# A fused attention and gated-MLP block: normalizing the first tokens on GpSimd, raw spatial weights on its queue, and one weight's parts made early

## The chip, the cores and the metric

The kernel runs on one NeuronCore of a Trainium2 chip. Its engines are TensorE (PE, with weight loads listed apart as PEld), VectorE (DVE), ScalarE (ACT), GpSimd (POOL) and SyncE (SP), which here only issues DMAs. The metric is the device time of one execution in microseconds (us), lower is better. It was 1884.51 us before the change: the median of 3 runs from 1882.85 to 1885.61.

## The reference

```python
x = A_x                                  # 1 x 2048 x 512, fp32
xn = layernorm(x)
# attention, 32 heads of 16
qkv = (xn @ wqkv) -> q, k, v
p = softmax(q k^T / sqrt(16));  a = (p v) @ wo
# gMLP, F = 1792, half 896
z = gelu(xn @ w_in);  z1, z2 = z[:, :896], layernorm(z[:, 896:])
g = w_sp @ z2 + b_sp[:, None]            # w_sp is 2048 x 2048
return x + a + (z1 * g) @ w_out
```

## The kernel before

All products are done with fp32 values split in two parts of a shorter format (the high part, a cast, and the low part, the rest after a subtraction), in three matmuls. Weights come as a raw fp32 tile by DMA, and `weight` makes the parts on GpSimd: `tensor_copy` (L282) and `tensor_sub` (L284). Parts, transposed x and other large tiles share a ring of 19 buffers ("big"); three more hold parts that are on their way out ("hilo").

**The start** is written out by hand. The 16 token tiles are four groups g. For each group `norm_x` computes mean and variance on DVE and normalizes in place (L327, ACT), `turn_x` transposes on PE (L333) and makes the parts xnT on ACT (L71) and DVE (L233), `qk_first` makes q and k of the first heads (L236 to L238), `v_tile` makes one token tile's v, and `load_stacks` loads q and k back in the layout of the scores. The parts of the v weights are cast by an early DMA and a DVE subtraction. xnT is stored to DRAM (xscr) by GpSimd's queue (L155).

**The loop** takes the 16 pairs of heads p, four column groups c and sixteen key tiles kt: 1024 steps. Each has a score matmul (S, L1095), its exponential on ACT (pf<-sl), a maxima matmul (M, L1109) for the next pair, its reduction on DVE (L811), and values (V, L1192), which come in blocks: after 8 scores, the 32 matmuls of 8 steps. There are 128 blocks. The gaps of PE are filled with dense work (D, L1154), two matmuls at a time on the two halves of the array, called a dense pair here. Where no dense work is ready, a filler pair (L1168) that computes nothing takes its place. The kind of pair is chosen by a planner at the end of the function, which runs when the program is built, has a clock of its own and writes out a fixed order for each engine:

```python
        queue = [v_rest(), qk_rest(), z2_all(), z1_all(), spatial(), mlp_out(), attn_out()]
        order = [(p, c, kt) for p in range(NP) for c in range(NG) for kt in range(NT)]
```

The dense queue is in that order: remaining v, remaining q and k, z2 and z1 of the gMLP, the spatial product (weights `wsp`, operand `zs` loaded from z2scr), the gMLP's output, and the attention's output (`op` and `ohl` from oscr, weights `wo`). Generators for the other engines yield an engine's letter ("G" for GpSimd) and an estimated time. `prepare` starts one `weight` per tile; `move` issues a DMA from SP, and `store` one from GpSimd in the start and from SP afterwards. `load_stacks` loads the next pair's q and k while no weights are owed, or from step LATE = 24 of a pair.

Of the kernel before, what the change touches and what calls it, by code (L numbers as in the profile page):

```python
# [16 lines left out]
P = 128  # L17
# [18 lines left out]
ZROOM = 4  # L36
LATE = 24
LEAD = 30
AGE = 6.0
GATED = "AD"  # L40
ORDER = ('SMDDSDDMDSDDMDDSDMDDSDMDDSDMDDSDMDDSDDMDMV', 'SMDDDDSDMDDSDMDDSDMDDSDMDDDSDMDDSDDDDMSV')
# [12 lines left out]
def fused_block(ctx, tc, x, wqkv, wo, w_in, w_spT, b_sp, w_out, out):  # L54
# [54 lines left out]
    escr = [[dr.tile([8, 2, 2, DH, 512], F32, name=f"escr{g}_{c}") for c in range(NG)] for g in range(4)]  # L109
    rscr = [[dr.tile([8, 512], F32, name=f"rscr{g}_{c}") for c in range(NG)] for g in range(4)]  # L110
    mscr = [dr.tile([4, 32, 32], F32, name=f"mscr{i}") for i in range(4)]
    bsplit = dr.tile([2, S], F32, name="bsplit")
    cscr = dr.tile([1, S], F32, name="cscr")
    bscr = [dr.tile([P, D], F32, name=f"bscr{t}") for t in range(NT)]
# [125 lines left out]
    def begin(nm, src, n, blocks=1, early=None):  # L240
# [10 lines left out]
        move(dst, src)  # L251
        if early:
            nc.gpsimd.dma_start(hi, src)
        return rw
# [7 lines left out]
            gps(1.3).tensor_sub(t[:, 1, :n], rw, t[:, 0, :n].bitcast(F32))  # L262
        return t

    def prepare(out, loads, spare=(0,)):
        for k, *a in loads:
            owed[0] += 1
            spawn(weight(out, k, a, spare), 1)

    raws = [0]  # L270
    owed = [0]

    def weight(out, k, a, spare):
        yield "C", lambda: raws[0] < DEEP and room["big"] > 1 + spare[0]
        raws[0] += 1
        rw = begin(*a)
        n = rw.shape[1]
        yield "T", LOAD
        yield open_("big")
        t = piece(a[0])  # L280
        yield "G", 0.61
        nc.gpsimd.tensor_copy(t[:, 0, :n], rw)  # L282
        yield "G", 0.0026 * n
        nc.gpsimd.tensor_sub(t[:, 1, :n], rw, t[:, 0, :n].bitcast(F32))  # L284
        raws[0] -= 1
        owed[0] -= 1
        lease("big", 1)
        yield "T", 0.02
        out[k] = t

    wq, w2, w1, wsp, wout, wo_ = {}, {}, {}, {}, {}, {}
# [15 lines left out]
    def norm_x(g, parts=1):  # L307


        mv = sm.tile([P, 4, 2], F32, tag="mv", name=f"mv{g}", bufs=2)  # L310
        rs = sm.tile([P, 2, 4], F32, tag="rs", name=f"rs{g}", bufs=2)
        k = 4 // parts
        for a in range(parts):
            tiles = range(a * k, (a + 1) * k)
            sl = slice(a * k, (a + 1) * k)
            for i in tiles:
                st = sm.tile([P, 6], F32, tag="bst", name=f"bst{g}_{i}", bufs=4)
                nc.vector.bn_stats(st, xs[g, i])
# [4 lines left out]
            nc.vector.scalar_tensor_tensor(rs[:, 1, sl], mv[:, sl, 0], -1.0, rs[:, 0, sl], ALU.mult, ALU.mult)  # L323
            for i in tiles:
                if i % 4 == 2:
                    yield
                nc.scalar.activation(xs[g, i], xs[g, i], AF.Identity, bias=rs[:, 1, i:i + 1], scale=rs[:, 0, i:i + 1])  # L327

    def turn_x(g):
        for c in range(ND):  # L330
# [209 lines left out]
    def z2_all():  # L540
        yield from need(lambda: len(w2) == 2 * ND)
        for t in range(NT):
            xt = xts.pop(t)
            if t + 2 < NT:
                yield from need(lambda: room["big"] > 1)
                z2_load(t + 2)
            if t == NT - 3:
                prepare(w1, [(f, f"w1_{f}", w_in[:, f * P:(f + 1) * P], D, ND) for f in range(NF)], spare=late1)
            if t == NT - 1:
                yield from need(lambda: room["big"] > 5)  # L550
                fetch_xnT(0)
# [47 lines left out]
    def z1_all():  # L599
        for g in range(NG):  # L600
# [55 lines left out]
    def spatial():  # L656
        for n, (g, (x, y)) in enumerate(units):
# [6 lines left out]
                load_b(g + 1)  # L664
            if lone:
                if g + 1 < NG:
                    prepare(wsp, [((g + 1, s), *sp_weights(g + 1, s)) for s in range(NT)])
                else:
                    prepare(wout, [(f, f"wout{f}", w_out[f * P:(f + 1) * P, :], 512) for f in range(NF)], spare=(2,))
            if not opens:  # L670
                yield "s",
            banks = (0, 1) if opens else (1, 0)
# [113 lines left out]
        lease("big", NF)  # L786

    stacks = [0]

    def load_stacks(p, cols=slice(0, S)):  # L790
        m, r = p // 4, (p % 4) * 2
# [43 lines left out]
    def norm_out(g4, c):  # L835
# [130 lines left out]
        for _ in gen:  # L966
            pass

    def init_rows(a):

        for j in range(2):
            row = 64 * j + KS
            for r in range(2):
                nc.gpsimd.dma_start(raw(kst[a])[row + r:row + r + 1, :], cscr[0:1, :])

    engines = {mybir.EngineType.PE, mybir.EngineType.Activation, mybir.EngineType.DVE, mybir.EngineType.Pool, mybir.EngineType.SP}
    with tc.manual_schedule(engines=engines):
        load_x(0)
        w0 = [piece(f"wqk0_{a}") for a in range(2)]
        w0r = [begin(*qk_weights(0, a), early=w0[a]) for a in range(2)]  # L980
        load_x(1)
        ones = t512("ones")
        nc.vector.memset(ones[0:32, 0:P], 1.0)
        wv, wvr = [], []
        for c in range(ND):
            t = (qst, kst)[c // 2][1].rearrange("p (b a f) -> p b a f", b=2, a=2)[:, c % 2]
            wv.append(t)
            wvr.append(begin(f"wv{c}", wqkv[c * P:(c + 1) * P, 2 * D:3 * D], 512, early=t))
        nc.gpsimd.dma_start(cscr.rearrange("o (a b) -> (o a) b", b=P), ones[0:16, 0:P])
        nc.gpsimd.memset(vhead[:, :, :, DH:], 1.0)  # L990
        nc.gpsimd.memset(vall[:, NT * H * (DH + 1):], 0.0)
# [3 lines left out]
        load_x(2)  # L995
        for r, t in zip(w0r, w0):
            end(r, t, True)
        turn_x(0)
        load_x(3)
        init_rows(0)  # L1000
        for r, t in zip(wvr, wv):
            end(r, t, True)
        norm = norm_x(1, 2)
        for g in range(NG):
            for _ in qk_first(g, w0):
                if g == 0:
                    next(norm, 0)
            load_stacks(0, slice(g * 512, (g + 1) * 512))
            for t in range(EARLY * g // NG, EARLY * (g + 1) // NG):
                v_tile(t, wv)  # L1010
            if g + 1 < NG:
                for _ in norm:
                    pass
                turn_x(g + 1)
                if g + 2 < NG:
                    norm = norm_x(g + 2)
                    next(norm)
# [4 lines left out]
        braw = t512("braw")[0:16, 0:P]  # L1022
        bhl = hilo("bhl")[0:16, :, 0:P]
        move(braw, b_sp)
        nc.vector.tensor_copy(bhl[:, 0, :], braw)
        nc.vector.tensor_sub(bhl[:, 1, :], braw, bhl[:, 0, :].bitcast(F32))
        for a in range(2):
            move(bsplit[a:a + 1, :], bhl[:, a, :])
# [53 lines left out]
        def scores():  # L1082
            nonlocal n_st
            p, c, kt = order[n_st]
            if n_st == 22:
                init_rows(1)
# [216 lines left out]
```

## Time and profile before

| | |
|---|---|
| runs | 1884.51 us median, 1882.85 to 1885.61 |
| profiled execution | 1888.93 us, span 1887.1 us, mean granted TensorE clock 0.989 |
| busy | PE 1825.1, DVE 1444.7, ACT 1225.3, POOL 690.7 us |
| filler matmuls (L1168) | 240, of PE's 14,812 |
| DMA | 291.47 MB, 154 GB/s on average |

The times of the trace are of the profiled execution. A row of its timeline gives the start and the length in us, the engine, the line, the operation, the tiles written and read, how many instructions it joins, and in brackets how long the engine was idle before it and what ended that. A row of a table of windows gives, for each engine, busy us and instructions, then the granted clock, the share of the DMA engines in use, and GB/s.

### The profile page before, as it was taken

To read this page: it belongs to the slowest core of one execution; us is meant where nothing else is said; L and a number is where in the kernel's file an instruction comes from. 1 tells how busy PE (TensorE), PEld (TensorE's weight loads), DVE (VectorE), ACT (ScalarE), POOL (GpSimd) and SP (SyncE) were. 2 spreads that over 40 slices of the span, in tenths; PEclk is the share of its full clock that TensorE was granted. 3 is DMA by queue.
4 is the path that set the end of the run, shared out by engine and by line. 5 is a ranking of instruction groups with operands and counts; after the bars stand their busy time and mean duration, and the time that the engine had idled before them with its cause. 6 is when DMAs were issued, how large, how long until landed. Compare 5 with 4: busy or idle time off the path is not lost.

```text
span 1887.1 us, 38105 instructions
## 1 busy us (share of the span) xinstructions
PE 1825.1 (97%) x14812; PEld 1109.3 (59%) x14812; DVE 1444.7 (77%) x1677; ACT 1225.3 (65%) x1338; POOL 690.7 (37%) x797
## 2 busy tenths in 40 slices
PE   6899999999998999999999999999999999999998
PEld 5665656566554656566655656565656565556554
DVE  5577878888876878778777877787778777878873
ACT  4247777888775777666656666666666665656555
POOL 2202142687886878800171217000722140002110
PEclk9899999999998999999999999999999999999999
DMA  9505573444455353474677657463787576456342
GB/s 329 208 3 170 203 225 111 98 137 118 133 160 160 129 130 110 141 167 119 158 201 194 165 142 227 133 148 103 219 194 160 161 201 145 124 140 174 116 129 92
DMA packets 208109, 291.47 MB, mean 154 GB/s; under 512 B 36008, under 2 KB 107368, under 8 KB 205048
## 3 DMA queue, kind: packets, MB, share of 16 engines
q1 hardware_dynamic: 197944, 258.03, 50.6%
q0 software_dynamic: 9984, 31.01, 4.8%
q8 instruction: 116, 1.90, 0.4%
q14 instruction: 65, 0.53, 0.1%
HBM read 186.98 MB, written 101.98 MB: 153 GB/s over the span
## 4 chain that ended last, share of the span: by engine, by line
PE 84%; DMA 4%; DVE 4%; POOL 4%; issue 2%; ACT 2%; SPq 0%; DVEq 0%; POOLq 0%; ACTq 0%
PE dps L1154 33%; PE sl L1192 22%; PE sl L1095 13%; PE sl L1109 12%; DVE mm L811 3%; DMA mscr<-ms 1%; PE dps L1168 1%; POOL wsp L284 1%; ACT pf L71 1%; DMA wqk<-in_wqkv 1%; PE sl L236 0%; PE sl L237 0%; DMA qst<-mscr 0%; PE sl L238 0%; ACT x L327 0%
## 5 line engine op out<-in xcount | busy, mean ns | idle before, releaser
L811 DVE TENSOR_REDUCE mm<-sl 128x2 f32<-128x1024 f32 x1024 | 1226.2, 1223 | 184.0 <-PE sl L1109 178.3
L71 ACT ACTIVATE pf<-sl 128x1024 f32<-128x1024 f32 x1024 | 1042.9, 1027 | 356.6 <-PE sl L1095 315.4
L1192 PE MATMUL sl<-pf,vall 128*32 128x512 f32 x4096 | 467.3, 597 | 0.0
L1095 PE MATMUL sl<-qst,kst 50*128 50x512 f32 x2048 | 441.4, 421 | 13.0 <-DVE mm L811 2.9
L1154 PE MATMUL dps<-wsp,zs 64*128 64x512 f32 x2688 | 441.4, 393 | 3.1 <-DMA zs<-z2scr 3.1
L1109 PE MATMUL sl<-kst,qst 48*128 48x512 f32 x2048 | 428.1, 408 | 7.2 <-DVE mm L811 3.5
L1095 PEld LDWEIGHTS sl<-qst,kst 50*128 50x128 f32 x2048 | 197.6, 185 | 223.8 <-issue 85.7
L1154 PEld LDWEIGHTS dps<-wsp,zs 64*128 64x128 f32 x2688 | 266.8, 187 | 41.5 <-DMA zs<-z2scr 3.7
L1192 PEld LDWEIGHTS sl<-pf,vall 128*32 128x32 f32 x4096 | 120.3, 110 | 270.6 <-issue 241.1
L1109 PEld LDWEIGHTS sl<-kst,qst 48*128 48x128 f32 x2048 | 197.6, 186 | 113.5 <-ACT pf L71 54.6
L1212 DVE TENSOR_TENSOR e<-sl,e 128x512 f32<-128x512 f32 x64 | 44.3, 692 | 174.3 <-PE sl L1192 133.8
L720 POOL TENSOR_TENSOR hhl<-z1i,hhl 128x512 fp32r<-128x512 f32 x28 | 35.8, 1290 | 332.3 <-ACT hhl L71 332.3
L71 ACT ACTIVATE e<-sl 128x512 f32<-128x512 f32 x64 | 38.3, 599 | 176.5 <-PE sl L1192 159.9
L1154 PE MATMUL dps<-w,xt 64*128 64x448 f32 x768 | 110.9, 369 | 2.3 <-ACT z L71 0.4
L1154 PE MATMUL dps<-wout,hp 64*128 64x512 f32 x672 | 111.5, 393 | 0.0
L858 POOL TENSOR_TENSOR ob<-ob 128x512 f32<-128x512 f32 (+1 forms) x16 | 20.6, 1288 | 181.9 <-DMA ob<-rscr 181.9
L1154 PEld LDWEIGHTS dps<-w,xt 64*128 64x128 f32 x768 | 73.9, 186 | 17.1 <-issue 8.0
L420 POOL TENSOR_TENSOR qkhl<-qr,qkhl 128x512 fp32r<-128x512 f32 x24 | 30.4, 1285 | 115.2 <-ACT qkhl L71 93.7
L1154 PEld LDWEIGHTS dps<-wout,hp 64*128 64x128 f32 x672 | 65.5, 187 | 9.1
L854 POOL TENSOR_TENSOR ob<-ob 128x512 f32<-128x512 f32 (+1 forms) x16 | 21.0, 1312 | 96.8 <-DMA ob<-escr 96.8
L1154 PE MATMUL dps<-xnT,wqk 64*128 64x512 f32 x288 | 47.4, 396 | 1.1 <-ACT vall L71 0.4
L1154 PE MATMUL dps<-wo,op 64*128 64x512 f32 x288 | 47.5, 407 | 0.6
(279 smaller groups left out, 1629.0 us busy)
## 6 DMA issues: line engine op xcount, KB each, us to landing
zs<-z2scr SPq DMA_DIRECT2D x192, 256.0 KB
escr<-e SPq DMA_DIRECT2D x60, 256.0 KB
hscr<-hhl POOLq DMA_DIRECT2D x28, 512.0 KB, 5.6
qst<-qscr SPq DMA_DIRECT2D x30, 384.0 KB
kst<-kscr SPq DMA_DIRECT2D x30, 384.0 KB
qscr<-qkhl SPq DMA_DIRECT2D x16, 512.0 KB
xscr<-xnT POOLq DMA_DIRECT2D x16, 512.0 KB, 4.5
kscr<-qkhl SPq DMA_DIRECT2D x16, 512.0 KB
```

The lines of the kernel that those rows point to most:

```text
L71: return nc.scalar.activation(out, in_, func, **kw)
L284: nc.gpsimd.tensor_sub(t[:, 1, :n], rw, t[:, 0, :n].bitcast(F32))
L420: nc.gpsimd.tensor_sub(hl[:, 1, :], raw_, hl[:, 0, :].bitcast(F32))
L720: nc.gpsimd.tensor_sub(hl[:, 1, :], z1, hl[:, 0, :].bitcast(F32))
L811: nc.vector.tensor_reduce(mmax[g][:, :, t, kc], sl[k], AX.X, ALU.max)
L854: nc.gpsimd.tensor_add(both_[rows, 0, :], both_[rows, 0, :], both_[rows, 1, :])
L858: nc.gpsimd.tensor_mul(both_[rows, 0, :], both_[rows, 0, :], both_[rows, 1, :])
L1095: nc.tensor.matmul(sl[k][:, j, :], kst[p % 2][rows, kt * P:(kt + 1) * P], qst[p % 2][rows, c * 512:(c + 1) * 512], start=True, stop=True)
L1109: nc.tensor.matmul(sl[k][:, j, :], qst[p % 2][rows, tt * P:(tt + 1) * P], kst[p % 2][rows, kc * 512:(kc + 1) * 512], start=True, stop=True)
L1154: nc.tensor.matmul(dps[:, bank, :w], lhs, rhs, start=go, stop=stop)
L1192: nc.tensor.matmul(sl[k][cols:cols + VW, 0, :], vpack(kt + r, 2 * p + j), pf[:, j * 512:(j + 1) * 512], start=n == n_pv, stop=n == n_pv + ...
L1212: nc.vector.tensor_add(e, sl[k][:, 0, :], e)
```

## The change

1. In the start GpSimd normalizes (`tensor_scalar`, L346 of the changed kernel). x of group 2 is loaded earlier. The transposes of a group stand right behind q and k of the group before; the v tiles come later, in shares of 0, 1, 2 and 1. The v weights' parts are made on GpSimd between the normalizations of groups 2 and 3. All 16 stores of xnT follow the last normalization. The b_sp split moves into the first group, and the initial rows of kst are written through SP.
2. The parts of the seven w1 weights are made when the loop begins, stored to w1scr, and fetched as parts (`fetch_parts`) near the end of z2.
3. The raw loads of the spatial weights of column groups 1 to 3, and of w_out, are issued on GpSimd's queue (`own`). In the planner a weight's cast and subtraction become one piece of work.
4. A flag `calm` keeps the stack loads out from the end of z2 to the first tile of z1 done, unless the pair is at step 24.
5. The move of the reciprocals to rscr is planned 1.5 instead of 0.3 us after it.

```diff
+AHEAD = (1,)
-    def weight(out, k, a, spare):
+    def weight(out, k, a, spare, own=False):
         yield "C", lambda: raws[0] < DEEP and room["big"] > 1 + spare[0]
         raws[0] += 1
-        rw = begin(*a)
+        if own:
+            lease("big", -1)
+            yield "G", 0.7
+            lease("big", 1)
+        rw = begin(*a, put=nc.gpsimd.dma_start if own else None)
...
-        yield "G", 0.61
+        yield "G", 0.61 + 0.0026 * n
         nc.gpsimd.tensor_copy(t[:, 0, :n], rw)
-        yield "G", 0.0026 * n
         nc.gpsimd.tensor_sub(t[:, 1, :n], rw, t[:, 0, :n].bitcast(F32))
...
+    def ahead_of_time(k, a, scr, spare):
+        out = {}
+        yield from weight(out, k, a, spare)
+        store(scr, out[k])
+        after(2.5, lease, "big", 1)
+
+    def fetch_parts(out, k, scr, spare):
+        yield "C", lambda: room["big"] > 1 + spare[0]
+        t = piece(f"wf{k}")
+        move(t, scr)
+        yield "T", LOAD
+        out[k] = t
...
-                nc.scalar.activation(xs[g, i], xs[g, i], AF.Identity, bias=rs[:, 1, i:i + 1], scale=rs[:, 0, i:i + 1])
+                nc.gpsimd.tensor_scalar(xs[g, i], xs[g, i], rs[:, 0, i:i + 1], rs[:, 1, i:i + 1], ALU.mult, ALU.add)
...
             if t == NT - 3:
-                prepare(w1, [(f, f"w1_{f}", w_in[:, f * P:(f + 1) * P], D, ND) for f in range(NF)], spare=late1)
+                calm[0] = False
+                for f in range(NF):
+                    spawn(fetch_parts(w1, f, w1scr[f], late1), 1)
...
+                if n == 1:
+                    calm[0] = True
...
-                    prepare(wsp, [((g + 1, s), *sp_weights(g + 1, s)) for s in range(NT)])
+                    prepare(wsp, [((g + 1, s), *sp_weights(g + 1, s)) for s in range(NT)], own=True)
...
-        after(0.3, move, rscr[g4][c][:nh].rearrange("h (b x) -> h b x", x=32), sums[rows, 1, :])
+        after(1.5, move, rscr[g4][c][:nh].rearrange("h (b x) -> h b x", x=32), sums[rows, 1, :])
...
+            run(qk_first(g, w0))
             load_stacks(0, slice(g * 512, (g + 1) * 512))
...
+            if g + 1 < NG:
+                turn_x(g + 1)
+            if g + 2 < NG:
+                run(norm_x(g + 2, 2))
+            if g == 0:
+                for r, t in zip(wvr, wv):
+                    end(r, t)
+            for t in ((), (0,), (1, 2), (3,))[g]:
                 v_tile(t, wv)
...
+        for f in range(NF):
+            owed[0] += 1
+            spawn(ahead_of_time(f, (f"w1_{f}", w_in[:, f * P:(f + 1) * P], D, ND), w1scr[f], AHEAD), 1)
...
-            if p + 1 < NP and stacks[0] <= p and i >= (3 if p else 20) and (not owed[0] or i >= LATE):
+            if p + 1 < NP and stacks[0] <= p and i >= (3 if p else 20) and (i >= LATE or calm[0] and not owed[0]):
```

On PE in the start of the kernel before, the last matmuls of the first group's v tiles (the v weights' parts lie in qst and kst) stand ahead of the transposes of the second group's x:

```order
L236 MATMUL sl_188<-kst_93,xnT_3_281 128x512
L237 MATMUL sl_188<-kst_93,xnT_3_281 128x512
L238 MATMUL sl_188<-kst_93,xnT_3_281 128x512
L333 MATMUL dps<-ident,x_0_203 128x128 x2
L333 MATMUL dps<-ident,x_2_204 128x128 x2
```

After the change, at the same place, the last matmuls for k of the first group (weights wqk_1) stand there:

```order
L238 MATMUL sl_194<-xnT_3_291,wqk_1_203 128x512
L239 MATMUL sl_194<-xnT_3_291,wqk_1_203 128x512
L240 MATMUL sl_194<-xnT_3_291,wqk_1_203 128x512
L352 MATMUL sl_195<-ident,x_0_210 128x128 x2
L352 MATMUL sl_195<-ident,x_2_211 128x128 x2
```

The v tiles have moved behind the transposes.

On GpSimd, where the spatial weights of the second column group begin, the kernel before has the parts of one weight after another, with the loads on SP:

```order
L854 TENSOR_TENSOR ob_0_9942<-ob_0_9942 128x512
L282 CAST wsp_0_10219<-wsp_0r 128x512
L284 TENSOR_TENSOR wsp_0_10219<-wsp_0r,wsp_0_10219 128x512
L282 CAST wsp_1_10225<-wsp_1r 128x512
L282 CAST wsp_2_10235<-wsp_2r 128x512
L284 TENSOR_TENSOR wsp_1_10225<-wsp_1r,wsp_1_10225 128x512
```

The changed one has, at the same place, the four loads ahead of the four casts and subtractions (ob and ohl are the attention's normalized rows):

```order
L253 DMA wsp_0r<-in_w_spT 128x512
L253 DMA wsp_1r<-in_w_spT 128x512
L253 DMA wsp_2r<-in_w_spT 128x512
L253 DMA wsp_3r<-in_w_spT 128x512
L882 TENSOR_TENSOR ob_0_9935<-ob_0_9935 128x512
L888 CAST ohl_0_10338<-ob_0_9935 128x512
L288 CAST wsp_0_10356<-wsp_0r 128x512
L289 TENSOR_TENSOR wsp_0_10356<-wsp_0r,wsp_0_10356 128x512
L288 CAST wsp_1_10368<-wsp_1r 128x512
L289 TENSOR_TENSOR wsp_1_10368<-wsp_1r,wsp_1_10368 128x512
```

The next four loads stand behind the four weights made from these.

On PE at the end of the kernel before, behind the last block of values (L1192), 22 dense matmuls of the attention's output are left (L949 and L934 belong to the last pair of heads):

```order
L1192 MATMUL sl_186<-pf_19966,vall 32x512 x2
L949 MATMUL sl_188<-sel,on_19882 128x512 x2
L949 MATMUL sl_187<-sel,on_19882 128x512 x2
L934 MATMUL sl_186<-e_3_19881,sel 32x128 x8
L1154 MATMUL dps<-wo_18280,op_1_19711 128x512 x4
L1154 MATMUL dps<-wo_18281,op_1_19711 128x512 x6
L1154 MATMUL dps<-wo_18300,op_1_19711 128x512 x6
L1154 MATMUL dps<-wo_18312,ohl_3_19765 128x512 x6
```

In the changed kernel the same stretch begins like this:

```order
L1212 MATMUL sl_193<-pf_19928,vall 32x512 x2
L1174 MATMUL dps<-wo_18763,op_0_19824 128x512 x6
L1174 MATMUL dps<-wo_18768,op_0_19824 128x512 x2
L958 MATMUL sl_194<-e_3_19808,sel 32x128 x8
L1174 MATMUL dps<-wo_18768,op_0_19824 128x512 x4
L1174 MATMUL dps<-wo_18791,op_0_19824 128x512 x6
L1174 MATMUL dps<-wo_18796,ohl_2_19231 128x512 x6
L1174 MATMUL dps<-wo_18763,op_1_19829 128x512 x6
```

In all, six half tiles of 24 dense matmuls stand behind its last values: 144, or 72 dense pairs, instead of 22, or 11 pairs. Counted over the whole order, it has 324 filler matmuls against 240. Its blocks of few dense pairs lie elsewhere: blocks 63 to 65 (counted from 0) have 9, 11 and 17 pairs where the kernel before has 24, 24 and 25; blocks 77 to 79 have 22, 12 and 12, blocks 93 to 95 have 9, 12 and 16. From block 123 to 127 it has 24 each, and the kernel before 17, 27, 4, 19 and 18. At the beginning of z1, blocks 30 to 34 have 11, 13, 24, 9 and 15 against 2, 22, 8, 16 and 24.

More of the change, by code (lines that the diff above doesn't have):

```diff
@@ L111, in fused_block @@
     mscr = [dr.tile([4, 32, 32], F32, name=f"mscr{i}") for i in range(4)]
+    w1scr = [dr.tile([P, 2, 512], F32, name=f"w1scr{f}") for f in range(NF)]
     bsplit = dr.tile([2, S], F32, name="bsplit")
@@ L238, in mm3, with begin @@
         nc.tensor.matmul(acc, lh, rl, start=False, stop=last)
-    def begin(nm, src, n, blocks=1, early=None):
+    def begin(nm, src, n, blocks=1, early=None, put=None):
         rw = piece(nm + "r").bitcast(F32)[:, 0, :n]
@@ L250, in begin @@
             hi = early[:, 0, :n]
-        move(dst, src)
+        (put or move)(dst, src)
         if early:
@@ L263, in end, with prepare @@
         return t
-    def prepare(out, loads, spare=(0,)):
+    def prepare(out, loads, spare=(0,), own=False):
         for k, *a in loads:
             owed[0] += 1
-            spawn(weight(out, k, a, spare), 1)
+            spawn(weight(out, k, a, spare, own), 1)
     raws = [0]
     owed = [0]
-    def weight(out, k, a, spare):
+    def weight(out, k, a, spare, own=False):
         yield "C", lambda: raws[0] < DEEP and room["big"] > 1 + spare[0]
         raws[0] += 1
-        rw = begin(*a)
+        if own:
[3 more added lines that the diff above has]
+        rw = begin(*a, put=nc.gpsimd.dma_start if own else None)
         n = rw.shape[1]
@@ L666, in spatial @@
                 if g + 1 < NG:
-                    prepare(wsp, [((g + 1, s), *sp_weights(g + 1, s)) for s in range(NT)])
+                    prepare(wsp, [((g + 1, s), *sp_weights(g + 1, s)) for s in range(NT)], own=True)
                 else:
-                    prepare(wout, [(f, f"wout{f}", w_out[f * P:(f + 1) * P, :], 512) for f in range(NF)], spare=(2,))
+                    prepare(wout, [(f, f"wout{f}", w_out[f * P:(f + 1) * P, :], 512) for f in range(NF)], spare=(2,), own=True)
             if not opens:
@@ L967, in run, with init_rows @@
             pass
-    def init_rows(a):
+    def init_rows(a, put):
         for j in range(2):
@@ L973, in init_rows @@
             for r in range(2):
-                nc.gpsimd.dma_start(raw(kst[a])[row + r:row + r + 1, :], cscr[0:1, :])
+                put(kst[a][row + r:row + r + 1, :], cscr[0:1, :])
     engines = {mybir.EngineType.PE, mybir.EngineType.Activation, mybir.EngineType.DVE, mybir.EngineType.Pool, mybir.EngineType.SP}
@@ L981, in fused_block @@
         load_x(1)
+        load_x(2)
         ones = t512("ones")
         nc.vector.memset(ones[0:32, 0:P], 1.0)
[L984 to L991, printed above, removed]
+        move(cscr.rearrange("o (a b) -> (o a) b", b=P), ones[0:16, 0:P])
+        wv = [(qst, kst)[c // 2][1].rearrange("p (b a f) -> p b a f", b=2, a=2)[:, c % 2] for c in range(ND)]
+        wvr = [begin(f"wv{c}", wqkv[c * P:(c + 1) * P, 2 * D:3 * D], 512) for c in range(ND)]
+        load_x(3)
+        braw = t512("braw")[0:16, 0:P]
+        bhl = hilo("bhl")[0:16, :, 0:P]
+        move(braw, b_sp)
+        init_rows(0, move)
         for r in (0, 64):
@@ L994, in fused_block @@
         run(norm_x(0, 2))
-        load_x(2)
+        turn_x(0)
         for r, t in zip(w0r, w0):
             end(r, t, True)
[L998 to L1003, printed above, removed]
+        run(norm_x(1, 2))
+        nc.gpsimd.memset(vhead[:, :, :, DH:], 1.0)
+        nc.gpsimd.memset(vall[:, NT * H * (DH + 1):], 0.0)
         for g in range(NG):
-            for _ in qk_first(g, w0):
-                if g == 0:
-                    next(norm, 0)
+            run(qk_first(g, w0))
             load_stacks(0, slice(g * 512, (g + 1) * 512))
-            for t in range(EARLY * g // NG, EARLY * (g + 1) // NG):
-                v_tile(t, wv)
[L1011 to L1017, printed above, removed]
+            if g == 0:
+                nc.vector.tensor_copy(bhl[:, 0, :], braw)
+                nc.vector.tensor_sub(bhl[:, 1, :], braw, bhl[:, 0, :].bitcast(F32))
+                for a in range(2):
+                    move(bsplit[a:a + 1, :], bhl[:, a, :])
+            if g + 1 < NG:
+                turn_x(g + 1)
+            if g + 2 < NG:
+                run(norm_x(g + 2, 2))
+            if g == 0:
+                for r, t in zip(wvr, wv):
+                    end(r, t)
+            for t in ((), (0,), (1, 2), (3,))[g]:
+                v_tile(t, wv)
         for g in range(NG):
@@ L1021, in fused_block @@
         steady.append(True)
[L1022 to L1028, printed above, removed]
         T.update(P=0.0, A=0.0, D=0.0, G=0.0)
@@ L1085, in scores @@
             if n_st == 22:
-                init_rows(1)
+                init_rows(1, move)
             i = n_st % 64
-            if p + 1 < NP and stacks[0] <= p and i >= (3 if p else 20) and (not owed[0] or i >= LATE):
+            if p + 1 < NP and stacks[0] <= p and i >= (3 if p else 20) and (i >= LATE or calm[0] and not owed[0]):
                 stacks[0] = p + 1
```

1 line of the change is left out of this document (added).

## The prediction

> **What bounds the kernel now.** I read the engines of the page first, then the waits and timeline of the start, then the stretches where TensorE is not fed, and last the end.
>
> ```profile
> PE 1825.1 (97%) x14812; PEld 1109.3 (59%) x14812; DVE 1444.7 (77%) x1677; ACT 1225.3 (65%) x1338; POOL 690.7 (37%) x797
> ```
>
> TensorE is busy 97% of the span, so only three kinds of thing can move the end: the rows in which it stands idle or at half clock, its instructions that do no work of the reference (filler), and the order in which scores and dense work share it. The loop repeats one block of 8 scores, some maxima, dense pairs (two half-height matmuls side by side) and the values of the scores. The first value matmul of successive blocks dates them. First a stretch of the second gMLP part:
>
> ```profile
> 557.11 3.64 PE L1192 MATMUL sl<-pf,vall 128*32 128x512 f32 x32
> 579.63 3.64 PE L1192 MATMUL sl<-pf,vall 128*32 128x512 f32 x32
> 593.24 4.99 PE L1192 MATMUL sl<-pf,vall 128*32 128x512 f32 x32
> 609.52 3.64 PE L1192 MATMUL sl<-pf,vall 128*32 128x512 f32 x32
> 622.81 3.64 PE L1192 MATMUL sl<-pf,vall 128*32 128x512 f32 x32
> 575.58 1.65 PE L1154 MATMUL dps<-xnT__5663,w 64*128 64x512 f32 x6 [4.44 <-ACT z L71]
> ```
>
> A block with 7 maxima takes 622.81 − 609.52 = 13.29. The three blocks before it took 22.52, 13.61 and 16.28, 52.41 together, and the first of them holds a wait of 4.44 for ACT. The next rows show why ACT was late: its buffer was held by the store at 568.62, which GpSimd issued late because it had made w1's parts just before. The DMA engines were also full and the clock half.
>
> ```profile
> 548.74 0.62 POOL L282 CAST w<-w_6r 128x512 fp32r<-128x512 f32 x1
> 549.32 1.30 POOL L284 TENSOR_TENSOR w<-w_5r,w 128x512 fp32r<-128x512 f32 x1
> 568.62 0.68 POOL L870 DMA_DIRECT2D oscr<-ohl  x1
> 574.93 0.60 ACT L71 ACTIVATE z<-dps 128x512 f32<-128x512 f32 x1 [5.21 <-issue]
> 565.00:570.00 5.00, 4.71 (x16) 2.04 (x16) 4.58 (x5) 3.74 (x5) 4.95 (x5) 0.53 0.99 197
> ```
>
> **The change part by part.** *Start.* The waits of TensorE between 20 and 75 us are few:
>
> ```profile
> PE sl L333 <- ACT x L327: 6.1, 8, 2.1
> PE dps L333 <- ACT x L327: 2.3, 3, 1.6
> 41.45 2.93 ACT L327 ACTIVATE x<-x,rs 128x512 f32<-128x512 f32 x4 [0.44 <-DVE rs L323]
> 60.00:65.00 5.00, 4.40 (x17) 3.92 (x18) 2.30 (x4) 3.41 (x6) 1.16 (x3) 0.51 0.36 117
> 74.40 1.65 PE L1154 MATMUL dps<-qst,xnT 64*128 64x512 f32 x12 [0.69 <-ACT vall L71]
> ```
>
> The transposes wait 6.1 + 2.3 = 8.4 us for the normalized x, because ACT normalizes a group only after it has copied out the q, k and v of the group before. The change gives that to GpSimd, which has little to do there, and issues the next transposes straight after q and k. One normalization costs about the same on either engine: 2.93 / 4 = 0.73 on ACT, 0.77 on GpSimd by a row of the same form:
>
> ```profile
> 532.40 0.77 POOL L523 TENSOR_SCALAR z<-z,zrs 128x512 f32<-128x512 f32 x1 [1.19 <-ACT z2hl L71]
> 129.73 1.98 POOL L974 DMA_DIRECT2D kst<-cscr  x4 [33.97 <-PE sl L1095]
> ```
>
> So the 8.4 us go. New is the split of the v weights on GpSimd, 4 × (0.62 + 1.30) = 7.7 us between the norms of groups 2 and 3; the v tiles are moved behind it, q and k of the next group cover it, and uncovered it costs up to 7.7. I put a new wait of 2.5 us on group 2's x, since its statistics come after the whole of group 1's (bounds 0 and 7.7). In the other direction, less idling leaves less half clock: at 0.51 in 60 to 65 that stretch did half its work, 2.5 us, and I take one such stretch as gone. Sum −8.4 + 2.5 − 2.5 = −8.4. The sixteen 512 KB stores of the transposed x, 8 MB, now leave GpSimd in one go after the last normalization, against four by four before, and meet the loads of the first score stacks; at the 197 GB/s of a full stretch they are 41 us of transfer. All of this gain could be lost in the first maxima's wait for those loads, so the bounds are −10 and 0.
>
> The seven w1 weights are split right after the loop's begin instead: 7 × 1.92 = 13.4 us of GpSimd, covered by its wait of 33.97 before 129.73. It costs nothing there; without that cover it would delay the next q and k splits by 13.4. The b_sp split, the initial rows by SP and the later move of the reciprocals have nothing waiting behind them that the rows show, and count zero.
>
> *The beginning of z1.* Three blocks of 9, 7 and 9 maxima at undisturbed speed take 13.86 + 13.29 + 13.86 = 41.0 (13.86 is a block with 9 maxima, quoted below), so 52.41 − 41.0 = 11.4 us are the stall. GpSimd loses 13.4 us of work there, and the stack loads stay out. Against that the fetch of finished parts is 7 × 512 KB instead of 7 × 256 KB, 1.8 MB more, which at 197 GB/s is 9 us of transfer in a stretch that is already full. I take 7.4 of the 11.4 as gained and 4 as staying, near the midpoint because rows speak for both (bounds −11.4, and +7 if the fetch is late for the first pair).
>
> *Spatial weights.* At the passage from the first to the second group of columns:
>
> ```profile
> 975.32 3.64 PE L1192 MATMUL sl<-pf,vall 128*32 128x512 f32 x32
> 986.76 0.50 PE L1154 MATMUL dps<-wsp,zs 64*128 64x512 f32 x1 [2.66 <-DMA zs<-z2scr]
> 994.62 3.64 PE L1192 MATMUL sl<-pf,vall 128*32 128x512 f32 x32
> 983.17 8.23 SPq L125 DMA_DIRECT2D zs<-z2scr  x6
> ```
>
> The block took 19.30, 5.4 over 13.86; TensorE waited for a z2 load that SP issued from 983.17 on. With the raw weights on GpSimd's queue SP is free earlier, and the planned order holds three passages with starved blocks (9, 11 and 17 dense pairs with filler, instead of 24). I count −4 (bounds −5.4 and +6). The Trainium skill, "Trainium Kernel Development and Optimization", section Key Constraints, speaks against this part: transfers from the SP and GpSimd queues share the same 16 DMA engines, and a second issuing engine saves only issue time. By it the term would be 0 and the sum 4 us later; the 8.23 us that six issues on SP took show issue time as well as transfer, and decide for me.
>
> A starved block costs nothing by itself, as two of the kernel before show, each with 7 filler pairs:
>
> ```profile
> 772.91 3.64 PE L1192 MATMUL sl<-pf,vall 128*32 128x512 f32 x32
> 785.58 3.64 PE L1192 MATMUL sl<-pf,vall 128*32 128x512 f32 x32
> 799.44 3.64 PE L1192 MATMUL sl<-pf,vall 128*32 128x512 f32 x32
> ```
>
> With 7 maxima it took 12.67, 0.6 less than 13.29; with 9 maxima 13.86. The order after has about four more such short blocks than before, 4 × 0.6, of which I count −2. The dense pairs that they displace aren't gone: they come at the end.
>
> *The end.* The last blocks and what follows them:
>
> ```profile
> 1802.96 3.64 PE L1192 MATMUL sl<-pf,vall 128*32 128x512 f32 x32
> 1817.46 3.64 PE L1192 MATMUL sl<-pf,vall 128*32 128x512 f32 x32
> 1836.01 3.64 PE L1192 MATMUL sl<-pf,vall 128*32 128x512 f32 x32
> 1846.69 3.64 PE L1192 MATMUL sl<-pf,vall 128*32 128x512 f32 x32
> 1859.39 3.64 PE L1192 MATMUL sl<-pf,vall 128*32 128x512 f32 x32
> 1871.09 3.64 PE L1192 MATMUL sl<-pf,vall 128*32 128x512 f32 x32
> 1876.31 2.12 PE L1154 MATMUL dps<-wo,op 64*128 64x512 f32 x16
> 1878.26 0.84 PE L1154 MATMUL dps<-wo,ohl 64*128 64x512 f32 x6
> ```
>
> Before, dense work runs dry here: blocks of 14.50 and 18.55 are 1.2 and 5.3 over 13.29, since the last attention rows aren't ready. After, the order has 24 pairs in each of them, work of earlier rows that nothing holds up; I count −4 of these 6.5 (bounds −6.5 and 0). The three blocks without maxima took 10.68, 12.70 and 11.70 with 12, 22 and 18 pairs (filler counted), about 0.2 a pair; with 24 each they take 12.70 + 2 × 0.2 = 13.1, together 39.3 instead of 35.1: +4.2. After the last values stood 11 pairs; now 72. Sixteen matmuls take 1878.26 − 1876.31 = 1.95, so a pair takes 0.24, and 61 more take +14.9. Four more half tiles are then evicted, partly beside the pairs; +1.1 for that gives +16 (bounds 14.9 and 20).
>
> The sum: −8.4 − 7.4 − 4 − 2 − 4 + 4.2 + 16 = −5.6. The profiled execution took 1888.93 (span 1887.1), so it would take 1883.3; it lies 4.4 above the median of the runs, 1884.51. For the median I take the same difference: 1884.5 − 5.6 = 1878.9, rounded 1879.
>
> **The rivals.** *Slower: the stall at z1's beginning stays and grows.* The fetched parts are issued on SP behind z2's stores and beside 2 MB of transposed x; GpSimd no longer being late doesn't help if the DMA engines (0.99) set the pace. Then −7.4 becomes 0 to +7, at its middle +3.5, and the sum −5.6 + 10.9 = +5.3: 1890. It decides as soon as the first z1 pair waits for its weight rather than for ACT. For it speaks the DMA share, against it the store at 568.62 that GpSimd, not DMA, made late.
>
> *The own queue brings nothing.* Raw loads land no sooner, GpSimd waits at each batch of four, and the z2 load is as late as before. The −4 falls away: −1.6, 1883, and up to 6 more if the later passages stall as the first did. This is the case that the Trainium skill's section Key Constraints, cited above, would give.
>
> *All stalls vanish.* −8.4 − 11.4 − 5.4 − 2 − 6.5 + 4.2 + 14.9 = −14.6: 1870. For it: each of these waits has its cause on an engine that the change relieves. Against it: dense work that is no longer late only empties the queue sooner.
>
> *The gain of the start doesn't arrive*, since the burst of 8 MB holds up the first stack loads: −8.4 becomes 0, the sum +2.8, 1887.
>
> **How the numbers follow.** About 0.2%, 3.8 us, is what a measurement of this kernel can tell from no change. Forecast 0.42 (its spread gives 0.25 faster, 0.11 same, 0.06 slower); z1's stall 0.22 (0.01, 0.03, 0.18); own queue 0.13 (0.02, 0.06, 0.05); all vanish 0.18 (all faster); start lost 0.05 (0.01, 0.02, 0.02). Together faster 0.47, same 0.22, slower 0.31. The range reaches from 1867, 3 below the case in which all vanishes, to 1893, 3 above the rival on the other side. The forecast's own range is 1874 to 1887: halfway to all its bounds below is 10.6 / 2 = 5.3, and above, where the far bounds are rivals of their own, a fifth of 40.8 is 8.2.
>
> **What would show it.** The first dense matmul of the loop should stand near 66 us and the first maxima near 72; the waits for x nearly gone. The three blocks at z1's beginning should take some 45 us. The passage between column groups should show no wait for z2 over 1 us. After the last values (1871.09 + 3.64 = 1874.7) stood 12.4 us up to the span's end; after the change some 28 should stand there. If the start isn't 5 us earlier, or the z1 pairs wait for a fetched weight, or the tail is under 22 us, the term named for it is wrong.

## The result and the profile after

The changed kernel is slower: 1903.51 us (median of 4 runs, 1902.88 to 1904.25) against 1885.06 for the kernel before on the same chip, a ratio of 1.0093 with a 95% interval of 1.008 to 1.0105. The forecast was 1879 with a range of 1867 to 1893. The profiled span is 1902.5, 15.4 longer than before; the medians differ by 18.5, since the profiled execution of the kernel before (1888.93) was one of its slower ones.

On the page of the changed kernel, the engines (busy us, share of the span, instructions), the filler matmuls among the groups of instructions, and the stores of the transposed x among the DMA issues, whose last number is the median time from issue to landing:

```profile
PE 1838.8 (97%) x14896; PEld 1104.3 (58%) x14896; DVE 1439.1 (76%) x1677; ACT 1210.4 (64%) x1324; POOL 735.7 (39%) x863
L1188 PE MATMUL dps<-brow,zeror 64*128 64x512 f32 x324 | 59.8, 395 | 1.0 <-ACT z L72 0.4
xscr<-xnT POOLq DMA_DIRECT2D x16, 512.0 KB, 13.1
```

TensorE is still busy 97% of a span that is now longer, so what was added isn't idle time alone. GpSimd has 45 us more.

**The start.** In the timeline of PE, the loop begins at 65.50 instead of 74.40, as forecast. The first maxima (L1129) come at 71.45, and then they stop:

```profile
65.50 1.65 PE L1174 MATMUL dps<-qst,xnT 64*128 64x512 f32 x12 [0.69 <-ACT vall L72]
...
71.45 0.87 PE L1129 MATMUL sl<-kst,qst 48*128 48x512 f32 x6
...
82.04 0.76 PE L1129 MATMUL sl<-kst,qst 48*128 48x512 f32 x1 [7.82 <-DMA kst<-kscr]
```

What they wait for stands in the chain of the first 130 us (start, length, what):

```profile
50.70 11.94 DMA kscr<-qkhl
...
70.02 9.73 DMA kscr<-qkhl
80.65 2.66 DMA kst<-kscr
```

Two stores of k took 11.94 and 9.73 us, and the load of the score stack could only follow. The sixteen stores of the transposed x had left GpSimd from 45.79 on. The windows show how full the DMA engines were, and how TensorE stood still afterwards (the last three columns are clock, share of the DMA engines, GB/s):

```profile
65.00:70.00 5.00, 4.41 (x36) 3.38 (x38) 0.00 (x0) 0.45 (x1) 0.00 (x0) 1.00 1.02 383
70.00:75.00 5.00, 3.74 (x32) 2.52 (x28) 3.09 (x3) 1.08 (x2) 0.00 (x0) 1.00 1.03 410
75.00:80.00 5.00, 0.00 (x0) 0.00 (x0) 0.40 (x1) 0.00 (x0) 0.00 (x0) 0.70 0.61 231
```

**z1's beginning.** The first value matmuls of the same three blocks, and the wait of the first late dense pair:

```profile
559.42 6.43 PE L1212 MATMUL sl<-pf,vall 128*32 128x512 f32 x32
...
589.16 0.80 PE L1174 MATMUL dps<-xnT__5718,wf 64*128 64x512 f32 x2 [3.83 <-ACT z L72]
...
608.63 3.64 PE L1212 MATMUL sl<-pf,vall 128*32 128x512 f32 x32
```

The three blocks took 49.2 us (52.4 before; 41.0 undisturbed). GpSimd's store, the cause before, is 11 us earlier, but ACT is late again, now for a buffer that a store of z2 holds, behind windows in which the DMA engines were full. That the full DMA engines made this store late is argued from these rows; no run isolates it.

```profile
557.24 0.71 POOL L894 DMA_DIRECT2D oscr<-ohl  x1
```
```profile
588.51 0.60 ACT L72 ACTIVATE z<-dps 128x512 f32<-128x512 f32 x1 [3.73 <-DMA z2scr<-z2hl]
```
```profile
575.00:580.00 5.00, 5.00 (x46) 1.82 (x42) 4.79 (x11) 3.06 (x5) 3.20 (x4) 1.00 1.06 287
580.00:585.00 5.00, 3.61 (x20) 1.42 (x16) 4.29 (x4) 4.23 (x5) 4.91 (x6) 1.00 1.03 182
```

The stack loads were to stay out of this stretch. They didn't:

```profile
568.11 0.45 SPq L127 DMA_DIRECT2D qst<-qscr  x1
...
572.82 0.42 SPq L127 DMA_DIRECT2D kst<-kscr  x1
```

The new flag has no effect in this kernel: the program that is built is the same without it.

**Behind the starved blocks.** Blocks 67 to 69, which the planner filled with 27 dense pairs to catch up, are dated by these four:

```profile
1041.64 3.64 PE L1212 MATMUL sl<-pf,vall 128*32 128x512 f32 x32
1056.70 3.64 PE L1212 MATMUL sl<-pf,vall 128*32 128x512 f32 x32
1070.86 3.64 PE L1212 MATMUL sl<-pf,vall 128*32 128x512 f32 x32
1084.89 1.50 PE L1212 MATMUL sl<-pf,vall 128*32 128x512 f32 x12
```

They took 15.06, 14.16 and 14.03; before, with 24 or 25 pairs, 13.16, 13.65 and 13.17. In all, nine blocks have 27 pairs from block 66 on and took 8.9 us more than the same blocks before, and the nine starved ones ahead of them took 2.5 us less. So the catch-up blocks give back more than the starved blocks save.

**The end.** The last value block and the last dense matmuls on PE, then the last work of DVE:

```profile
1869.43 3.64 PE L1212 MATMUL sl<-pf,vall 128*32 128x512 f32 x32
...
1888.71 2.37 PE L1174 MATMUL dps<-wo,op 64*128 64x512 f32 x18 [1.32 <-DVE fin L925]
...
1894.02 0.85 PE L1174 MATMUL dps<-wo,ohl 64*128 64x512 f32 x6
```
```profile
1896.06 2.35 DVE L980 TENSOR_TENSOR fin<-sl,fin 128x1024 f32<-128x1024 f32 x2
```

From that block's start to the end of the span it is 33.0 us, against 1887.1 − 1871.09 = 16.0 before: +17.0 for 61 more dense pairs.

### The profile page after: what moved, and what is told of

It is laid out like the page before. It is cut to its first block, busy times and chain, and to the rows that moved or that the text cites. A ratio compares the mean times of both kernels' runs of the same rounds, so it can differ in the third digit from the quotient of the medians.

```text
span 1902.5 us, 38263 instructions
## 1 busy us (share of the span) xinstructions
PE 1838.8 (97%) x14896; PEld 1104.3 (58%) x14896; DVE 1439.1 (76%) x1677; ACT 1210.4 (64%) x1324; POOL 735.7 (39%) x863
## 4 chain that ended last, share of the span: by engine, by line
PE 87%; DVE 4%; DMA 4%; POOL 2%; issue 2%; ACT 1%; SPq 1%; DVEq 0%; ACTq 0%; POOLq 0%
PE dps L1174 35%; PE sl L1212 23%; PE sl L1115 14%; PE sl L1129 12%; DVE mm L835 3%; PE dps L1188 2%; DMA kscr<-qkhl 1%; DMA z2scr<-z2hl 1%; SPq L127 1%; DMA zs<-z2scr 0%; DMA kst<-kscr 0%; DMA oscr<-ohl 0%; DMA mscr<-ms 0%; ACT pf L72 0%; POOL wsp L289 0%
## 5 line engine op out<-in xcount | busy, mean ns | idle before, releaser
L1129 PE MATMUL sl<-kst,qst 48*128 48x512 f32 x2048 | 426.5, 408 | 15.6 <-DMA kst<-kscr 8.4
L1174 PE MATMUL dps<-wsp,zs 64*128 64x512 f32 x2688 | 436.3, 392 | 1.2 <-DMA zs<-z2scr 0.7
L1174 PEld LDWEIGHTS dps<-wsp,zs 64*128 64x128 f32 x2688 | 261.7, 187 | 43.7 <-DMA zs<-z2scr 1.9
L1129 PEld LDWEIGHTS sl<-kst,qst 48*128 48x128 f32 x2048 | 196.1, 185 | 125.4 <-ACT pf L72 64.3
L1188 PE MATMUL dps<-brow,zeror 64*128 64x512 f32 x324 | 59.8, 395 | 1.0 <-ACT z L72 0.4
## 6 DMA issues: line engine op xcount, KB each, us to landing
xscr<-xnT POOLq DMA_DIRECT2D x16, 512.0 KB, 13.1
```

The costliest lines, as they stand in the source:

```text
L1129: nc.tensor.matmul(sl[k][:, j, :], qst[p % 2][rows, tt * P:(tt + 1) * P], kst[p % 2][rows, kc * 512:(kc + 1) * 512], start=True, stop=True)
L1174: nc.tensor.matmul(dps[:, bank, :w], lhs, rhs, start=go, stop=stop)
L1188: nc.tensor.matmul(dps[:, bank, :], zeror[r:r + 64], brow[r:r + 64], start=not begun, stop=not begun)
```

## The experiments

All times are medians of 5 to 11 runs beside runs of the kernel before on the same chip, and the ratio is to those. The runs were taken on several chips, so a difference of two medians from different runs is less sure than that of their ratios. "First values" is the start of the first L1192 matmul or its counterpart (124.2 in the kernel before, 126.5 in the changed one), "tail" the time from the start of the last value block to the end of the span.

**1. Stores of the transposed x by group.** In the changed kernel:

```diff
             load_stacks(0, slice(g * 512, (g + 1) * 512))
+            for c in range(ND):
+                store(xscr[g][c], xnT[g, c])
...
-        for g in range(NG):
-            for c in range(ND):
-                store(xscr[g][c], xnT[g, c])
```

> The changed kernel, with the stores of each group's transposed x to DRAM issued in the start right after that group's q and k and stack loads (four by four), instead of all sixteen behind the last normalization. Nothing else moves; the loop's order is the same. Theory A (the burst of 16 stores holds up the q and k stores and the stack loads that the first maxima wait for): the loop still begins near 65.5 us, the first late maxima wait less than 1 us instead of 7.8 and 0.5, the first values come some 9 us earlier, and the time falls by 8 to 10 us against the changed kernel, to about 1894. Rival B (the first stack loads are slow whatever else moves, because q and k are ready only shortly before): the wait stays over 5 us and the time within 3 us of 1903.5.

Measured: 1892.64 us, ratio 1.0034 (1.0022 to 1.0046), 10.9 us under the changed kernel. The loop begins at 65.11, the maxima no longer wait, and the first values stand at 115.3, 11.2 earlier. Two rows of PE:

```profile
65.11 1.65 PE L1173 MATMUL dps<-qst,xnT 64*128 64x512 f32 x12 [0.69 <-ACT vall L72]
...
73.66 0.77 PE L1128 MATMUL sl<-kst,qst 48*128 48x512 f32 x2
```

Theory A holds: the burst alone cost more than the whole gain of the start. The DMA engines are nearly as full without it (0.95 in the window from 65 to 70); what is gone is the burst just ahead of the last q and k stores. SP begins to issue the last stores of k at 64.99 and the load that waits for them at 70.01, 5.0 us later; in the changed kernel these are 68.57 and 79.80, 11.2 apart.

**2. Raw loads back on SP.** In the changed kernel:

```diff
-                    prepare(wsp, [...], own=True)
+                    prepare(wsp, [...])
-                    prepare(wout, [...], spare=(2,), own=True)
+                    prepare(wout, [...], spare=(2,))
```

> The changed kernel, with the raw loads of the spatial weights and of w_out back on SP's queue. Its order has no dense pair left after the last block of values (72 in the changed kernel). Theory A (the loads on GpSimd's queue make the weights come in batches, which leaves dense pairs for the end and makes catch-up blocks of 27 pairs): from the last values to the end 12 us remain instead of 29.6, and the time falls by 17 to 22 us against the changed kernel, to 1882 to 1887. Rival B (the displaced pairs come back as longer blocks, since each pair must be done somewhere): the tail shrinks, but the blocks grow by as much, and the time falls by less than 6 us.

Measured: 1887.65 us, ratio 1.0011 (1.0001 to 1.0022), 15.9 under the changed kernel: a little less than theory A's 17 to 22, and far from B's 6. The tail is 17.0 us (33.0). New waits appear in the loop, in blocks 77 and 91; the seventh run is about them.

**3. Both.** The two edits together.

> Both of the edits of the two runs before together: stores of the transposed x by group, raw loads on SP. If the two costs lie in different places and add: 1903.5 less 9 less 19, 1873 to 1878, faster than the kernel before by 0.4 to 0.6%. If they don't add (an earlier loop only meets the z1 stall and the passages earlier): over 1880.

Measured: 1877.47 us, ratio 0.9959 (0.9946 to 0.9972), 26.0 under the changed kernel where the single edits gave 10.9 and 15.9. They add, within the intervals.

**4. Both, with w1 raw and late again,** and without the flag (which moves nothing):

```diff
-                for f in range(NF):
-                    spawn(fetch_parts(w1, f, w1scr[f], late1), 1)
+                prepare(w1, [...], spare=late1)
```

> The same, and besides the w1 weights are again loaded raw and split on GpSimd near the end of z2, without the flag that keeps the stack loads out: so the start and the merged piece of work are what is left of the change. Theory A (making w1's parts early shortens the stall at z1's beginning by 3 to 8 us, as the blocks there show: 2.6 us in the changed kernel): 3 to 8 us slower than the run with both edits. Rival B (the fetch of finished parts costs in transfers what it saves on GpSimd): within 2 us of it.

Measured: 1876.53 us, ratio 0.9951 (0.9939 to 0.9963): the same within the intervals. The five blocks 30 to 34 took 78.3 instead of 74.9, so making the parts early does shorten the stall, but the lead was gone by block 63, where the third run waited longer. Rival B by the total time, A at its place.

**5. The new start alone** in the kernel before, with spread stores.

> The kernel before with the new start alone (normalization on GpSimd, transposes straight behind q and k, v tiles later), its stores of the transposed x spread by group as in the first run. The loop's order is that of the kernel before. Theory A (the start's gain is independent of the loop): the first values come 9 to 10 us earlier than in the kernel before and nothing later gives it back: 1874 to 1877. Rival B (the loop's stalls at z1, at the passages and near the end meet the same transfers and only move): the gain shrinks to under 6 us by the last values, 1880 or more.

Measured: 1878.53 us, ratio 0.9967 (0.9955 to 0.9979), 6.0 under the kernel before. In the traces the first values come 8.5 earlier and the last value block 8.8 earlier (1862.27 against 1871.09), so nothing later gives the gain back: theory A for the place. The size lies between the two theories: 8.5 in place of 9 to 10, and a time between A's 1874 to 1877 and B's 1880; it is 6.0 by the medians and 8.4 by the two spans.

**6. The same compute order, other queue.** The first run, with `put=None` for the raw loads: SP issues them, and GpSimd's booked 0.7 us stay in the plan.

> The changed kernel with spread stores, and the raw spatial and w_out loads issued by SP, at the same places of the planned order at which GpSimd would have issued them: the compute order is unchanged, with its starved blocks and the 72 pairs behind the last values; only the queue differs. Theory A (the place in the order costs the time, not the queue): within 3 us of the run with spread stores, 1892.6. Rival B (GpSimd's queue itself is slow, or its issue holds GpSimd up): 5 us or more faster than that.

Measured: 1892.71 us, ratio 1.0047 (1.0035 to 1.0059), against 1892.64 and 1.0034: theory A. Once the order is fixed, the queue that carries the loads makes at most a small difference: 0.1 us by the medians, 2.5 by the ratios, whose intervals overlap. The Trainium skill, "DMA: Bandwidth & Descriptors", section Issuing engines are not separate DMA queues, says that a second issuing engine saves only issue time. This run is in line with that. In the traces blocks 62 and 63 together took 31.3 us here and 29.3 in the first run, so a gain of some 2 us at that passage isn't excluded.

**7. Cast and subtraction as two pieces** again, spread stores, raw loads on SP, w1 early:

```diff
-        yield "G", 0.61 + 0.0026 * n
+        yield "G", 0.61
         nc.gpsimd.tensor_copy(t[:, 0, :n], rw)
+        yield "G", 0.0026 * n
```

> The changed kernel with spread stores, raw loads on SP, and cast and subtraction planned as two pieces again; w1's parts still made early, stack loads kept out. Its spatial part has the order of the kernel before. Theory A (the merged piece made the waits for z2 at blocks 77 and 91, up to 6.5 us each, which the kernel before doesn't have): these blocks return to 13.2, the waits are gone, and it is 1 to 6 us faster than the run with both edits, 1872 to 1876. Rival B (the early w1 or the reciprocals' later move made them): they stay, and the time stays within 1 us of 1877.5.

Measured: 1874.95 us, ratio 0.9952 (0.994 to 0.9965). Block 91 took 13.18 where the third run has this:

```profile
1357.12 3.64 PE L1211 MATMUL sl<-pf,vall 128*32 128x512 f32 x32
...
1363.36 0.47 PE L1173 MATMUL dps<-wsp,zs 64*128 64x512 f32 x1 [1.93 <-DMA zs<-z2scr]
...
1377.10 3.64 PE L1211 MATMUL sl<-pf,vall 128*32 128x512 f32 x32
```

That is 19.98 us, with a wait for z2. So the merged piece, with the loads on SP, does make the waits (block 77 goes from 17.48 to 13.19 too). But block 62 goes the other way, from 14.25 to 18.84, and with block 63 the two are 0.9 us longer. In the total, 2.5 us, the intervals of the two runs overlap.

**8. Own loads with two pieces.** The first run with the edit of the seventh; 48 pairs are left for the end.

> The changed kernel with spread stores and cast and subtraction planned as two pieces, the raw loads still on GpSimd's queue. Its order leaves 48 dense pairs for the end (72 with the merged piece, 11 without own loads). Theory A (what own costs is the pairs left over, some 0.24 us each and a hand-over per half tile): between the runs with and without them, some 6 us under the run with spread stores, 1885 to 1888. Rival B (the loads on GpSimd's queue cost in the loop, not at the end): within 2 us of 1892.6.

Measured: 1886.59 us, ratio 1.0008 (0.9999 to 1.0017): theory A. With the seventh and the first run it gives the price of a pair left over. Tails of 16.1, 26.4 and 33.0 us belong to 11, 48 and 72 pairs: 10.3 / 37 = 0.28 and 6.6 / 24 = 0.28 us a pair, the copies of the results included.

**9. The seventh run with w1 raw and late** (the edit of the fourth).

> The run with two pieces (1874.95), with w1 again loaded raw and split near the end of z2; all else stays. Theory A (making w1's parts early is what takes 4.4 us out of the five blocks at z1's beginning, 74.95 against 79.50 with the new start alone): these five blocks take 79 to 80 again and the time rises by 3 to 5 us, to 1878 to 1880. Rival B (the gain is given back later, as it was between the third and the fourth run): the blocks take longer but the time stays within 1.5 us of 1875.

Measured: 1877.49 us, ratio 0.995 (0.9936 to 0.9965), against 0.9952. The five blocks took 78.9 instead of 74.9, as theory A said; the time lies between the two theories. By the ratios it is the same, by the spans (1875.4 and 1872.3) 3.1 longer. What w1's early parts are worth in the whole stays open between 0 and 3 us.

**10. The loads on GpSimd's queue without a booked turn.** The seventh run with `own=True`, and

```diff
         if own:
-            lease("big", -1)
-            yield "G", 0.7
-            lease("big", 1)
+            pass
```

> The run with two pieces (1874.95), with the raw loads of the spatial weights of the later groups and of w_out issued on GpSimd's queue, without the 0.7 us that the planner books on GpSimd for each: its PE order is that of the run with two pieces, with 11 dense pairs left at the end. Theory A (the booked turn on GpSimd, not the queue, made the changed kernel slow): 1872 to 1877, no slower than with SP's queue. Rival B (GpSimd's own issue, some 0.55 us each, holds up what stands behind it): over 1879. Theory C, the purpose of that part of the change (SP is free for the z2 loads): the passage at block 62 shrinks from 18.84 to under 16, and the time by 2 us or more.

Measured: 1894.53 us, ratio 1.0044 (1.0031 to 1.0056): rival B, and against theory A, on which I had counted. The PE order is that of the seventh run. On GpSimd each load stands between casts and subtractions, takes 0.56 us, and some wait 0.30 for their buffer, so what stands behind them comes later. Here that is z1i, which ACT needs ahead of its next exponentials; a row of POOL's loads, z1i, ACT, and on PE the stand-still that follows:

```profile
1157.23 0.56 POOL L253 DMA_DIRECT2D wsp_11r<-in_w_spT  x1 [0.30 <-POOL wsp L288]
1157.82 1.29 POOL L732 TENSOR_TENSOR z1i<-z1i,z1b 128x512 f32<-128x512 f32 x1
```
```profile
1159.14 0.63 ACT L72 ACTIVATE hhl<-z1i 128x512 fp32r<-128x512 f32 x1 [2.57 <-POOL z1i L732]
```
```profile
1160.73 0.80 PE L1127 MATMUL sl<-kst,qst 48*128 48x512 f32 x2 [2.06 <-ACT pf L72]
```

GpSimd begins z1i 6.5 us after the block's first values (1157.82 − 1151.34); in the seventh run 2.6 (1145.14 − 1142.50), and there ACT doesn't wait for it. Blocks 75 and 76 took 16.98 and 16.05 (13.19 and 13.80 in the seventh run), blocks 89 and 90 much the same, and block 62 21.80 instead of 18.84, so theory C falls too. So the loads cost time either way: booked in the plan, 11 to 16 us (eighth against seventh run, second against the changed kernel), as pairs left for the end; not booked, 17 (by the ratios) to 20 us, as waits of TensorE.

The third, fourth, seventh and ninth versions, at 0.995 to 0.996 of the kernel before, can't be told apart. The new start alone, at 0.9967, accounts for most of their gain; its interval overlaps theirs.

## Why the prediction was wrong

Measured between the same value blocks of the two traces, the steps came out like this (the sum is that of the profiled spans, 3.1 under the difference of the medians):

| step | forecast | measured | |
|---|---|---|---|
| start, to the first values | −8.4 | +2.3 | 10.7 off |
| z1's beginning, blocks 30 to 40 | −7.4 | −1.7 | 5.7 off |
| passages and starved blocks, 47 to 101 | −4 − 2 | −0.3 | 5.7 off |
| blocks 123 to 127 | −4 + 4.2 | −1.5 | 1.7 better |
| tail | +16 | +17.0 | 1.0 off |
| the rest | 0 | −0.4 | |
| sum | −5.6 | +15.4 | |

**The start.** The waits for x went, the loop began at 65.50 (forecast "near 66"), the first maxima at 71.45 (72). The step that failed is that the sixteen stores of 8 MB count as nothing in the sum: that the gain "could be lost" to them stood in the text with its mechanism, but only as a bound and as a rival with a chance of 0.05 and a price of 8.4. It happened, and cost 11.2, more than the gain. The chance was low for what the working itself said, 41 us of transfer that meet the loads of the first score stacks. The figure was too large: the full windows of the changed kernel's start, from 50 to 75, moved 374 to 410 GB/s, not 197, so the 8 MB are an estimated 20 to 22 us, and they left from 45.79 on, 20 us before the loop. The signs named for this term, the loop at 66 and the first maxima at 72, both came true and didn't show its loss, because the wait comes a few maxima later. The first run shows the mechanism by removing it, and the fifth shows that the rest of the term was right: without the burst the start gains 8.5.

**z1's beginning.** Relieving GpSimd did what was said (its store came 11 us earlier), but the step "the stack loads stay out" rested on a flag that changes no instruction, and the 4 of 11.4 us that I left as staying were 8.2 (49.2 − 41.0). With the start mended, the seventh run has 4.5 of the 11.4 us (blocks 30 to 34, 74.95 against 79.50 in the fifth). The wait passed from one buffer of ACT to the next, which a z2 store held. The rival named transfers as the new limit here, at +0 to +7; the pairs waited for ACT and not for the weights, and what made the z2 store late stays argued.

**Passages.** "A starved block costs nothing by itself" was right, and so was 0.6 us less with 7 maxima. What the sum left out is the other side of the order: the nine blocks with 27 pairs, +8.9 us. The gain at the passages was there (block 62 16.1 instead of 19.3) and went into these blocks. It doesn't follow the queue, to which the forecast put it down. Block 62 took 14.2 to 16.5 in all six traces with the merged piece, on either queue, and 18.7 to 21.8 in all six with two pieces, the eighth run with its loads on GpSimd included (18.9).

**The end and the tail** came out about as worked out: 0.28 us a pair with all that belongs to it, against 0.24 and 1.1 us for evictions, and the 5.3 us stall of block 124 gone (13.1). This was the largest term of the sum and the one read from rows of the order and the trace together.

**The queue.** I let the 8.23 us that six issues took on SP decide against the rule of the Trainium skill, "Trainium Kernel Development and Optimization", section Key Constraints. The row was misread. SP's own waits in the kernel before, from 983 to 991.5, and in the tenth run, from 1157.9 to 1176, are these (us in total, times, the longest):

```profile
SPq L125 <- POOL wsp L284: 6.3, 2, 3.5
```
```profile
SPq L127 <- DMA wsp_13r<-in_w_spT: 8.6, 1, 8.6
SPq L127 <- POOL wsp L286: 7.3, 1, 7.3
```

The six issues took 4.5 us together, and 3.5 us of the 8.23 SP stood waiting for GpSimd's subtraction (L284), with another wait for it just ahead. So SP wasn't short of time. With 55 loads fewer on it, in the tenth run, a row of four z2 issues even lasts 17.88 us, of which the issues are 2.4 and the rest is such waits. The sixth run bears the rule out within its interval: the same order takes about the same time with the loads on either queue. The forecast took −4 from this part; it is the part that made the tail.

The forecast was on the wrong side because the start's gain was lost behind stores that the change itself had moved there (DMA share 1.02), because only a part of the gain at z1 came, in a stretch that its own rows showed as full (0.99), and because one term, the catch-up blocks, was missing.

## What to carry to other kernels

Where stores that nobody needs soon are moved into one place, look at what is queued behind them and when it is first waited for: the bytes are the same, but here the first loads behind them paid. Where a planner moves work from a full stretch to another, count both: the blocks that lose it, the blocks that catch up, and what is left when the rest has ended. A load issued by an engine that also computes took a turn of that engine here; it cost either that turn in the plan or, where the plan didn't know of it, a delay of what stood behind it. And a long row of issues on a queue isn't yet a busy queue: look at what it waited for.

## What the runs showed of the hardware

GpSimd normalizes as fast as ACT here: two 128 x 512 tiles in 1.52 us on either, four in 3.02 and 2.93. A 512 KB store on its queue landed in 4.5 us (median) when each group's four left as they became ready, in 7.1 when they left four at a time in the new start, and in 13.1 when all sixteen left in one go, the first nine in 4.84 us. Raw loads moved from SP's queue to GpSimd's at the same places of the order changed the time by 0.1 to 2.5 us (the sixth run), but put into GpSimd's stream without a planned turn they cost 17 to 20 us (the tenth).
